# Two turns of the merge go ahead of the turns of the next unit's B and K on VectorE

## The chip, the cores and the metric

The kernel runs on one core of a Trainium2 chip. The metric is the device time of one execution in microseconds (us): 1092.59, the median of three runs (1092.51 to 1094.92).

The core's engines run side by side, each through its own queue of instructions in order: TensorE (PE in the profile; its weight loads are PEld), VectorE (DVE), ScalarE (ACT), GpSimd (POOL) and SyncE (SP), which issues nearly all DMAs. Semaphores tie them together.

## The reference

A recurrence over time steps (an attention block of 4 batches, 8 heads, 768 steps, head size 40), and behind it a mixture of four experts over all tokens:

```python
for t in range(S):
    y[:, :, t] = np.einsum('bhd,bhde->bhe', rt, state)
    Sa = np.einsum('bhde,bhe->bhd', state, at)
    state_decay = state * wt[:, :, None, :] - np.einsum('bhd,bhe->bhde', Sa, bt)
    state = state_decay + np.einsum('bhd,bhe->bhde', vt, kt)
...
x = attn_out.transpose(0, 2, 1, 3).reshape(B * S, H * D)      # 3072 tokens of 320
for e in range(E):                                            # 4 experts, F = 1024
    out += p[:, e:e + 1] * (np.maximum(x @ w1[e], 0.0) @ w2[e])
```

All data are 32-bit floats.

## The kernel before

**Units.** The recurrence is done in chunks of 64 steps. A unit is one chunk of one pair of batches, 16 heads at once; there are 12 chunks and 2 pairs, so 24 units, 0 to 23. Within a unit everything that doesn't depend on the state is made ahead (`within`, `substitute`, `merge`), and `step` then takes the state through. The mixture of the tokens of finished units is cut into pieces (`mix`, `gap`) that lie between the parts of the recurrence on TensorE and keep it busy. From unit 8 on (`BY_CHANNEL = 8`) B and K are loaded "raw", heads along the partitions, and VectorE turns them itself.

**What a unit does, in the order of its names.** G is the decay's running product (a turn of raw W at line 513, a scan at line 559), gp its reciprocal (line 575). AT is A turned (line 617) and multiplied by G (line 619); VT and RT are V and R turned (line 535). NT and KT are B and K turned (line 631, in two halves each; the turn itself is line 318) and multiplied by gp (lines 633 and 637). `pg` takes gp to another layout (line 641). `pc` is the product of V and R, masked into VC (line 492, called from line 604). `pfe` (line 656) is the product of NT and AT and gives F; `pe` (line 669) that of KT and AT. F holds triangular systems. `substitute` puts F's blocks into one tile and turns them into M (line 726), and GpSimd then solves by substitution in Z, in 16 rounds of one product and two sums (lines 756 and 773), some 50 instructions in a row. `merge` turns Z into Qc (line 784) and Qc into QTc (line 785), both on VectorE; GpSimd copies QTc into QT (line 791); TensorE makes `pY` from QTc (line 811) and, from its result and Qc, `pQ` (line 814), which completes QT. `step` begins with `prn` (products with the state; RH is added from it, line 835) and goes on with `psat`, which reads QT and RH.

**In TensorE's order**, which is that of the program, a late unit u has: `pg` and `pc` of unit u + 1; `pY` of unit u; `prn` of unit u; a piece of the mixture's first layer (`ph`); `pQ` of unit u; more of the mixture; `pfe` of unit u + 1; mixture, with `psat` and the rest of the step of u between.

**The mixture's buffers.** `ph` (first layer, two tiles) and `p` (second layer, `p431`, `p75`, `p26`) share three PSUM tiles (tag "mm"). ScalarE takes `ph` out as `hs` (line 969), VectorE adds halves of `hs` into sums `a` (line 1095) and takes `p` out into `osb` (lines 982 and 984). The recurrence's products share five PSUM tiles (tag "big").

**What sets the order on VectorE.** Instructions are placed by a scheduler that goes by readiness, program order and priority (`sooner` raises it, and VC has it raised from unit 7 on). `keep` holds an instruction in program order among those that are kept; Qc, QTc, the blocks, M and Z's first products on VectorE are. On top stand edges between named instructions: `noted` gives an instruction a name, and a list of pairs at the end (lines 1426 to 1435) says which of two goes first on VectorE, without a semaphore. The turns of B and K (line 631) have no name before the change; the products of K have ("K8" to "K23"). In program order the turns of B and K of unit u + 1 stand ahead of Qc of unit u, with pieces of the mixture between.

The lines that the change touches, and two that the steps need:

```python
                    turn_raw(t[:, i::2], n["raw" + x][:, NJ * i:NJ * i + NJ])                 # 631
        keep(noted(nc.vector.transpose(out=dealt(Qc[:]), in_=q.Z), "Qc", q.u))                # 784
    ahead_of_merge = [(f"K{u}", f"Qc{u - 1}") for u in range(BY_CHANNEL, NU)]                 # 1430
    ahead_of_merge += [(f"QTc{u - 1}", f"RH{u - 1}.{r}") for u in range(BY_CHANNEL, NU) for r in range(2)]
    ahead_of_merge += [(f"QTc{u - 1}", f"VC{u}.{r}") for u in range(BY_CHANNEL, NU) for r in range(2)]
```

Of the kernel before, what the change touches and what calls it, by code (L numbers as in the profile page):

```python
# [33 lines left out]
def kernel(  # L34
# [46 lines left out]
    NJ = H // 2  # L81
    NF = F // P
    NU = NC * B // 2
# [6 lines left out]
    def noted(ins, name, n=None, i=None):  # L90
        if n is None:
            n = sum(k.startswith(name) for k in made)
        key = f"{name}{n}" if i is None else f"{name}{n}.{i}"
        made[key] = ins
        if key in names:
            stated_order.append(ins)
        return ins
# [89 lines left out]
    def kept(name, shape, n, value=0.0, eng=nc.gpsimd, lo=0):  # L187
        tiles = []
        for i in range(n):
            t = const.tile(shape, FP32, name=f"{name}{i}")  # L190
            eng.memset(t[:, :, lo:shape[2]], value)
            tiles.append(t)
        turn = [0]

        def take():
            turn[0] += 1
            return tiles[(turn[0] - 1) % n]

        return take
# [6 lines left out]
    BY_CHANNEL = 8  # L206
    padded = {}
    for n, a_sum in enumerate(("a1", "a7", "a5", "a2")):
        t = padded["RV"[n % 2], n // 2] = sb.tile([P, H, 64], FP32, name="padded", tag=a_sum)
        nc.gpsimd.memset(t[:, :, D:64], 0.0)  # L210
    PAD = D + D - Q
    raw = {x: kept(f"raw{x}", [P, 2 * NJ, 2 * D], 1, float(x == "W"), nc.vector, PAD) for x in "WARV"}
# [103 lines left out]
    def turn_raw(out, t):  # L316

        return nc.vector.transpose(  # L318
            out=out.rearrange("p n (x two) -> p n two x", two=2),
            in_=t.rearrange("p n (two e) -> p n two e", two=2)[:, :, :, 0:Q],  # L320
        )
# [172 lines left out]
    def within(q):  # L494

        n = q.n
# [129 lines left out]
        if by_channel:  # L626
            NT = sb.tile([P, 2 * NJ, L], FP32, name="NT", tag="turned", bufs=3)
            KT = sb.tile([P, 2 * NJ, L], FP32, name="KT", tag="turned", bufs=3)
            for t, x in ((NT, "B"), (KT, "K")):
                for i in range(2):  # L630
                    turn_raw(t[:, i::2], n["raw" + x][:, NJ * i:NJ * i + NJ])
                if x == "B":
                    nc.vector.scalar_tensor_tensor(
                        out=t[:], in0=t[:], scalar=-1.0, in1=gp[:], op0=ALU.mult, op1=ALU.mult,
                    )
                else:
                    noted(nc.vector.tensor_tensor(out=t[:], in0=t[:], in1=gp[:], op=ALU.mult), "K", q.u)
# [569 lines left out]

    in_order[0] = True
    ws = [within(units[u]) for u in range(3)]
    norm = normalize()  # L1210
    keep_warm(16)
# [80 lines left out]
    substitute(units[2], nc.gpsimd)  # L1292
    mix(1)
    ws.append(within(units[3]))
    run(ws[3], 1)

# [5 lines left out]
    for u in range(1, NU):  # L1302
        in_order[0] = True
        q = units[u]
# [70 lines left out]
        if early:  # L1375
            run(m, 1)
        else:
            run(m, 1)
            run(s_next, 1)
            lead()  # L1380
            run(m, 1)
            if u + 3 < NU:
                ws.append(within(units[u + 3]))
                run(ws[u + 3], 1)
# [42 lines left out]
    turned_ahead = [("Qc6", "RT7"), ("RT7", "QTc6")]  # L1427
    turned_ahead += [("QTc6", x) for x in ("VC7.0", "VC7.1", "sum_w15", "sum_w16")]
    waits_of_scalar = [(f"SXc0.{n}", "RTc1.0") for n in range(4)]
    ahead_of_merge = [(f"K{u}", f"Qc{u - 1}") for u in range(BY_CHANNEL, NU)]  # L1430
    ahead_of_merge += [(f"QTc{u - 1}", f"RH{u - 1}.{r}") for u in range(BY_CHANNEL, NU) for r in range(2)]
    ahead_of_merge += [(f"QTc{u - 1}", f"VC{u}.{r}") for u in range(BY_CHANNEL, NU) for r in range(2)]
    in_second = [("Zr1.14", "out0"), ("out0", "Zm1.16")]
# [32 lines left out]
```

## Time and profile before

| | us |
|---|---|
| median of three runs | 1092.59 (1092.51 to 1094.92) |
| the profiled execution's own time | 1093.63 |
| its span, first to last instruction | 1091.9 |
| PE busy | 1055.7 (97%) |
| DVE busy | 797.3 (73%) |
| POOL busy | 524.4 (48%) |
| ACT busy | 343.8 (31%) |
| mean granted clock of TensorE, as a share of full speed | 0.998 |

How to read it: times in the views are microseconds from the span's start. A line of the timeline gives start, duration, engine, line of the kernel, operation, what is written from what, and behind "x" how many instructions are merged in it; in brackets stands the time that the engine was idle before it and what released it. A line of the waits gives the engine and what it wanted to run, what it waited for, the microseconds in sum, how often, and the longest. Ends of matmuls are modelled and overlap. The stage that the change touches runs from about 270 us (the merge of unit 7) to about 925 us (that of unit 22); a unit takes some 43 us there. From 965 us on only the mixture is left but for the last steps.

### The profile page before, as it was taken

To read this page: it belongs to the slowest core of one execution; us is meant where nothing else is said; L and a number is where in the kernel's file an instruction comes from. 1 tells how busy PE (TensorE), PEld (TensorE's weight loads), DVE (VectorE), ACT (ScalarE), POOL (GpSimd) and SP (SyncE) were. 2 spreads that over 40 slices of the span, in tenths; PEclk is the share of its full clock that TensorE was granted. 3 is DMA by queue.
4 is the path that set the end of the run, shared out by engine and by line. 5 is a ranking of instruction groups with operands and counts; after the bars stand their busy time and mean duration, and the time that the engine had idled before them with its cause. 6 is when DMAs were issued, how large, how long until landed. Compare 5 with 4: busy or idle time off the path is not lost.

```text
span 1091.9 us, 38473 instructions
## 1 busy us (share of the span) xinstructions
PE 1055.7 (97%) x16012; PEld 946.9 (87%) x16012; DVE 797.3 (73%) x1565; ACT 343.8 (31%) x942; POOL 524.4 (48%) x1312
## 2 busy tenths in 40 slices
PE   8999999999999999999999999999999999999998
PEld 7787878889889889898888898888988989988888
DVE  7886679897878877868868778678687786543343
ACT  3433344422333323323233333232333332321110
POOL 5116777756366364463572653643735537430000
PEclk9999999999999999999999999999999999999999
DMA  6775643435434453452463453443444443121220
GB/s 119 197 212 114 140 108 107 104 76 112 117 85 102 102 115 91 110 120 62 93 147 71 94 148 65 105 113 85 108 95 109 99 99 95 51 71 56 76 82 13
DMA packets 275989, 111.04 MB, mean 102 GB/s; under 512 B 230456, under 2 KB 255592, under 8 KB 275816
## 3 DMA queue, kind: packets, MB, share of 16 engines
q1 hardware_dynamic: 271832, 107.76, 41.7%
q8 instruction: 126, 2.06, 0.8%
q10 hardware_dynamic: 3984, 0.84, 0.4%
q14 instruction: 47, 0.39, 0.1%
HBM read 100.65 MB, written 3.93 MB: 96 GB/s over the span
## 4 chain that ended last, share of the span: by engine, by line
PE 62%; DVE 14%; POOL 12%; issue 4%; DMA 3%; SPq 3%; ACT 1%; DVEq 0%; POOLq 0%; ACTq 0%
PE ph L110 26%; PE p L110 23%; POOL Z L773 8%; POOL Z L756 4%; PE pdy L110 2%; DVE osb L984 2%; DVE M L726 2%; PE po L110 2%; PE prn L110 1%; PE psat L110 1%; PE pxr L110 1%; DVE a L1095 1%; PE pfe L110 1%; PE pY L110 1%; DVE KT L318 1%
## 5 line engine op out<-in xcount | busy, mean ns | idle before, releaser
L773 POOL TENSOR_TENSOR Z<-Z 128x31 f32<-128x31 f32 (+7 forms) x704 | 258.4, 367 | 55.1
L110 PE MATMUL ph<-xT,w1a 128*128 128x256 f32 (+3 forms) x1536 | 222.8, 374 | 2.8 <-DMA w1a<-in_moe_w_dram 2.0
L110 PE MATMUL ph<-xT,w1b 128*128 128x256 f32 (+3 forms) x1536 | 223.7, 374 | 1.5 <-DVE a L1095 0.5
L1095 DVE TENSOR_TENSOR a<-hs 128x512 f32<-128x512 f32 x220 | 152.2, 710 | 91.8 <-ACT hs L969 91.8
L969 ACT ACTIVATE hs<-ph 128x512 f32<-128x512 f32 (+1 forms) x208 | 116.8, 564 | 324.3 <-PE ph L110 323.9
L110 PEld LDWEIGHTS ph<-xT,w1a 128*128 128x128 f32 (+1 forms) x1536 | 169.4, 161 | 31.8 <-issue 9.0
L110 PEld LDWEIGHTS ph<-xT,w1b 128*128 128x128 f32 (+1 forms) x1536 | 169.9, 161 | 29.0 <-issue 6.4
L756 POOL TENSOR_TENSOR Z<-M,Z 128x62 f32<-128x62 f32 (+7 forms) x352 | 148.6, 422 | 79.7 <-DVE M L742 53.9
L984 DVE SCALAR_TENSOR_TENSOR osb<-p,gate,osb 128x320 f32<-128x320 f32 (+1 forms) x243 | 108.2, 483 | 84.0 <-PE p L110 80.0
L110 PE MATMUL p<-sums,a 128*128 128x160 f32 x1056 | 164.9, 299 | 0.0
L110 PEld LDWEIGHTS p<-sums,a 128*128 128x128 f32 x1056 | 152.8, 190 | 2.2
L719 POOL COPY below<-F 32x256 f32<-32x256 f32 x48 | 22.9, 478 | 201.9 <-ACT F L662 189.7
L110 PEld LDWEIGHTS p<-w,hs 128*128 128x128 f32 x704 | 98.6, 190 | 8.7 <-issue 7.5
L110 PE MATMUL p<-w,hs 128*128 128x160 f32 x704 | 104.9, 302 | 0.1
L110 PE MATMUL p<-w,a 128*128 128x160 f32 x704 | 102.8, 299 | 0.0
L110 PEld LDWEIGHTS p<-w,a 128*128 128x128 f32 x704 | 98.0, 190 | 0.0
L791 POOL COPY QT<-QTc 32x256 f32<-32x256 f32 x96 | 40.3, 420 | 99.2 <-DVE QTc L785 94.2
L889 ACT COPY RS<-pxr 64x256 f32<-64x256 f32 x88 | 32.2, 366 | 100.3 <-DVE SX L492 73.6
L575 DVE RECIPROCAL gp<-G 128x512 f32<-128x512 f32 x16 | 53.6, 3352 | 0.5
L700 ACT COPY EV<-pev 64x160 f32<-64x160 f32 x96 | 23.1, 286 | 83.5 <-PE pev L110 83.1
L726 DVE STREAM_TRANSPOSE M<-blocks 128x1024 f32<-128x1024 f32 x24 | 47.7, 1986 | 1.9 <-ACT blocks L714 0.3
L662 ACT COPY F<-pfe 128x256 f32<-128x256 f32 x48 | 15.6, 376 | 79.3 <-PE pfe L110 78.1
(167 smaller groups left out, 1420.6 us busy)
## 6 DMA issues: line engine op xcount, KB each, us to landing
w1a<-in_moe_w_dram SPq DMA_DIRECT2D x37, 512.0 KB
w1b<-in_moe_w_dram SPq DMA_DIRECT2D x37, 512.0 KB
w<-in_moe_w_dram SPq DMA_DIRECT2D x4, 1280.0 KB
w1a<-in_moe_w_dram SPq DMA_DIRECT2D x74, 64.0 KB
w1b<-in_moe_w_dram SPq DMA_DIRECT2D x74, 64.0 KB
out_dram<-osb SPq DMA_DIRECT2D x45, 80.0 KB
rawW<-in_w_dram SPq DMA_DIRECT2D x48, 72.0 KB
natV<-in_v_dram SPq DMA_DIRECT2D x42, 80.0 KB
```

What stands on the lines that cost most here:

```text
L110: return stated(nc.tensor.matmul(**k))
L575: pin(noted(nc.vector.reciprocal(out=gp[:], in_=G[:, :, 1:L + 1]), "1/gp", q.u))
L700: nc.scalar.copy(out=of_slot(q.EV[half(p)], i ^ p)[:, :, 0:D], in_=pev[i][half(p)])
L719: tc.keep_in_program_order(nc.gpsimd.tensor_copy(out=q.below[quarter(i)], in_=q.F[quarter(i), :, 0:Q]))
L726: ins = nc.vector.transpose(out=M[:], in_=cols)
L756: ins = eng.tensor_tensor(out=Z[:, 1:3, 0:n, j + 1:Q], in0=M[:, j:j + 2, None, j + 1:Q].to_broadcast([P, 2, n, m]), in1=Z[:, here, 0:n, j: ...
L773: eng.tensor_tensor(out=z[:, 0], in0=z[:, 0], in1=z[:, x], op=ALU.add)
L791: ins = nc.gpsimd.tensor_copy(out=q.QT[quarter(i), :, quarter(i % 2)], in_=QTc[quarter(i)])
L889: nc.scalar.copy(out=RS[half(s), x ^ s::2], in_=prs[x][half(s)].rearrange("p (j i) t -> p j i t", i=2),)
L969: ins = nc.scalar.activation(out=h[:, i * HF // 2:(i + 1) * HF // 2, 0:n], in_=ph[i][:], func=ACTF.Relu,)
L984: ins = nc.vector.scalar_tensor_tensor(out=to, in0=p, scalar=sc, in1=to, op0=ALU.mult, op1=ALU.add)
L1095: ins = nc.vector.tensor_tensor(out=t[:], in0=x, in1=y, op=op)
```

## The change

From unit 8 on, the four turns of a unit's raw B and K get names, Br8.0, Br8.1, Kr8.0, Kr8.1 and so on. The edge that put K's product of unit u ahead of Qc of unit u − 1 is taken out. Edges that put QTc of unit u − 1 ahead of the four turns of unit u are put in. The products of B and K follow their turns by their data. The edges from QTc to RH and VC stay.

```diff
             for t, x in ((NT, "B"), (KT, "K")):
                 for i in range(2):
-                    turn_raw(t[:, i::2], n["raw" + x][:, NJ * i:NJ * i + NJ])
+                    noted(turn_raw(t[:, i::2], n["raw" + x][:, NJ * i:NJ * i + NJ]), x + "r", q.u, i)
...
-    ahead_of_merge = [(f"K{u}", f"Qc{u - 1}") for u in range(BY_CHANNEL, NU)]
+    ahead_of_merge = [(f"QTc{u - 1}", f"{x}r{u}.{i}") for u in range(BY_CHANNEL, NU) for x in "BK" for i in range(2)]
     ahead_of_merge += [(f"QTc{u - 1}", f"RH{u - 1}.{r}") for u in range(BY_CHANNEL, NU) for r in range(2)]
     ahead_of_merge += [(f"QTc{u - 1}", f"VC{u}.{r}") for u in range(BY_CHANNEL, NU) for r in range(2)]
```

## The prediction

> **What bounds the kernel now.** I read the page's busy shares first, then the chain that ended last, then what TensorE (PE) waited for.
>
> ```profile
> PE 1055.7 (97%) x16012; PEld 946.9 (87%) x16012; DVE 797.3 (73%) x1565; ACT 343.8 (31%) x942; POOL 524.4 (48%) x1312
> ...
> PE 62%; DVE 14%; POOL 12%; issue 4%; DMA 3%; SPq 3%; ACT 1%; DVEq 0%; POOLq 0%; ACTq 0%
> ```
> PE is busy nearly throughout, yet only 62% of the chain is PE: VectorE (DVE) and GpSimd (POOL) hold 26%, so a serial ring through them is close behind. The waits of PE, longest first:
>
> ```profile
> PE pY L110 <- DVE QTc L785: 16.9, 16, 1.4
> PE pdy L110 <- issue: 2.1, 1, 2.1
> ```
> One wait stands out: pY, the first product of the merge, waits for the turn QTc, 16 times. One is unit 0's (0.41 us); the others are units 7 to 21, 16.5 us in sum: 0.79 and 1.40 in units 7 and 8, 1.07 to 1.30 in the thirteen after. **16.5 us is the ceiling** of what the change can take away. The timelines of DVE, then PE, around unit 14's merge:
>
> ```profile
> 575.66 0.67 DVE L984 SCALAR_TENSOR_TENSOR osb<-p,gate,osb 128x160 f32<-128x160 f32 x2
> 576.25 0.76 DVE L318 STREAM_TRANSPOSE NT<-rawB 128x256 f32<-128x256 f32 x2
> 577.04 0.69 DVE L633 SCALAR_TENSOR_TENSOR NT<-NT,gp 128x512 f32<-128x512 f32 x1
> 577.65 0.77 DVE L318 STREAM_TRANSPOSE KT<-rawK 128x256 f32<-128x256 f32 x2
> 578.45 0.69 DVE L637 TENSOR_TENSOR KT<-KT,gp 128x512 f32<-128x512 f32 x1
> 579.06 0.61 DVE L784 STREAM_TRANSPOSE Qc<-Z 128x256 f32<-128x256 f32 x1
> 579.71 0.45 DVE L785 STREAM_TRANSPOSE QTc<-Qc 128x256 f32<-128x256 f32 x1
> 580.07 0.74 DVE L492 COPY_PREDICATED VC<-mask_up,pc 128x256 f32<-128x256 int32 x2
> 581.48 0.71 DVE L318 STREAM_TRANSPOSE AT<-rawA 128x512 f32<-128x512 f32 x1 [0.67 <-PE prn L110]
> ```
> ```profile
> 580.29 0.59 PE L110 MATMUL pY<-QTc,below 64*64 64x64 f32 x13 [1.08 <-DVE QTc L785]
> ...
> 591.17 0.69 PE L110 MATMUL pfe<-NT,AT 40*64 40x64 f32 x32
> 591.68 1.10 PE L110 MATMUL ph<-xT,w1b 64*64 64x256 f32 x16
> ```
> PE's product pc ended at 579.21 and PE stood 1.08 until QTc was there. DVE was not idle: it ran the six operations on B and K (576.25 to 579.06, 2.81 us) ahead of Qc, though POOL had ended Z at 574.40. From 581.48 on, DVE runs without a pause to the M turn (594.32).
>
> **The change, part by part.** No instruction is added or removed, and no DMA, POOL, PE or ScalarE instruction is moved. Two kinds of edges on DVE change: Qc no longer stands behind the K product, and the four turns of B and K stand behind QTc. So 2.81 us of DVE work go from in front of Qc/QTc (1.09 us from Qc's start to QTc's end) to behind them, in 16 units.
>
> *Gain at pY.* Without that work Qc may start at the end of the four osb additions or at the end of Z, whichever is later. In unit 14: Qc 576.25, QTc ends 577.34, pY can start 0.14 later (as 580.29 after 580.15) and is then held by pc, 579.21. The 1.08 go. In units 7 and 8 Qc already waited 1.03 us for Z, so nothing is gained there; in 9 to 21 it is at most 14.3 us.
>
> *What the turns cost behind QTc.* NT is read by pfe, 12 us after QTc, KT by pe, 20 us after; both are far enough. The raw buffers come free 1.1 us later, but SyncE issues the next load into them long after (522.80 against the turn at 488.64), so that costs nothing; a load that lands late costs less than before, since its turn is later (unit 13's K turn waited 0.13 us). What matters is the rest of DVE's queue: VC, AT, RH, G, scan, 1/gp, the hidden-state sums and the two p75 osb additions stand behind the turns. PE's first ph product after pfe needs PSUM that those two additions release: they end at 591.06 and ph starts at 591.68, so 0.5 us are in hand after the 0.13 of the signal. PE now comes 1.08 earlier; DVE comes 0.67 earlier, because the wait of AT for prn is covered by the turns. 0.5 + 0.67 − 1.08 is about 0.1: unit 14 gains its whole 1.08, and nothing is left over. **Any wait of DVE at Qc for Z therefore comes back at ph.**
>
> *Whether Qc waits for Z.* In unit 15 it does. POOL's timeline:
>
> ```profile
> 619.17 0.52 POOL L773 TENSOR_TENSOR Z<-Z 128x8 f32<-128x8 f32 x2
> 623.13 1.73 POOL L791 COPY QT<-QTc 32x256 f32<-32x256 f32 x4 [3.45 <-DVE QTc L785]
> ```
> Z ends at 619.68, the osb additions at 619.18. After the change unit 15's M turn comes 0.67 earlier with DVE, so Z ends at 619.01, while PE and the additions come 1.08 earlier (618.10). Qc starts at 619.05, 2.86 before its old 621.91; the turns behind it and the vanished AT wait give 2.81 − 0.67 = 2.14 back; the p75 additions end 0.72 earlier, at 633.20, and ph starts at 633.30 instead of 634.53: 1.23 earlier in all, 0.15 of it unit 15's own. Unit 16: Z 0.72 earlier (661.20), Qc 661.24, 3.67 earlier, additions 1.53 earlier, ph 2.05 earlier: 0.82 of its own. The other even units (10 to 20) keep 0.8 to 1.14 in the same way. So a pair of units gains about **1.0 us, not 2.2**, and 10 to 21 are six pairs: −6.0 us.
>
> *The start of the stage loses.* In units 7 and 8 Qc is released by Z, so the ring Z → Qc → QTc → DVE's queue → M → Z is the bound, and the turns are now inside it:
>
> ```profile
> 274.91 0.62 DVE L784 STREAM_TRANSPOSE Qc<-Z 128x256 f32<-128x256 f32 x1 [1.03 <-POOL Z L773]
> 275.56 0.45 DVE L785 STREAM_TRANSPOSE QTc<-Qc 128x256 f32<-128x256 f32 x1
> 275.93 0.74 DVE L492 COPY_PREDICATED VC<-mask_up,pc 128x256 f32<-128x256 int32 x2
> 277.87 0.32 DVE L835 TENSOR_TENSOR RH<-prn,EV 128x160 f32<-128x160 f32 x1 [1.21 <-PE prn L110]
> ```
> Only the 1.21 us before RH cover 2.81: M of unit 8, and so Qc 8, comes 1.6 us later. Unit 8 adds another 1.6, less the 0.95 that Qc 9 used to start after Z's end: Qc 9 is 2.3 late. In unit 9 the 2.14 of the turns stand against a slack of 1.07: ph 3.5 us late.
>
> **Sum:** +3.5 − 6.0 + about 0.2 in units 11 and 22 = −2.3 us. The profiled execution took 1093.63 (span 1091.9); that is 1.04 above the median of the runs shown, 1092.59. 1093.63 − 2.3 = 1091.3, by the median **1090.3 us**. Bounds: VC's place is unknown, and whether the other waits of PE at ph (0.27 to 1.30 us in the six odd units 9, 11, 13, 17, 19 and 21, put down mostly to DMAs of w1) move along: I let them move with the unit before. If they don't bind at all, −4.0; if AT's turn falls behind the p75 additions, as it stood in units 7 and 8, −5.0.
>
> A rule weighed here: POOL's pair of Z additions at 128x69 took 0.74 us (at 602.98) and the one at 128x68 took 1.26 (at 606.97), when DVE began the sums of two inputs. The Trainium skill, "SBUF — State Buffer", section "Who interferes with whom", says that a VectorE instruction with two SBUF inputs contends with GpSimd's reads. By that rule the N product (0.69) leaves Z's tail in units 9, 11 and 13, where Z ended during or just after it, and N falls on the QT copies instead, which is against the change, though psat reads QT only 12 us later. By the rule, as an estimate, the sum would be −2.3 less up to three times 0.7, −4.4; by the rows alone it is −2.3.
>
> **Rivals.**
> 1. *VC stands right behind QTc (slower).* VC reads pc. The stated edges put VC behind QTc but not behind the turns, and VC has a raised priority. pc now ends 1.9 us after QTc (579.21 against 577.34), so with less than 1.9 us of turns between them DVE waits for PE. Placed in front of all six, VC starts 0.15 after pc, the p75 additions end 0.15 + (591.06 − 580.07) − 0.67 + 2.81 = 13.28 after pc, ph starts at 13.4 instead of 12.47: +0.93 a unit in 10 to 21, some of it inside the DMA waits: with the start +13: 1105.6. For it: the priority. Against: pc isn't ready when QTc ends, so a placement by readiness takes the turns first.
> 2. *VC amid the turns, behind N.* It still waits a little, and a pair gains about 0.5: the start is just paid back, +0.8: 1093.4.
> 3. *The cover holds.* Free DVE operations are placed anew, ph is not held and units 7 and 8 lose little: up to −14.3: 1078.3. For it: DVE is idle 27% of the span. Against: from 581.48 to the M turn it isn't idle at all.
> 4. *Nothing changes*, because the new names don't bind: the key made of "Br", the unit and the half is the one that the edges use, so I give this almost nothing.
>
> **How the numbers follow.** Forecast 0.40, rival 1 0.27, rival 2 0.18, rival 3 0.15 (rival 4 within the second). A measurement tells 0.3% (3.3 us) from no change. Faster by more: rival 3 and 0.13 of the forecast (its lower end): 0.28. Slower by more: rival 1 and 0.02 of rival 2: 0.29. Within: 0.43. The range reaches from a partly held cover (1082) to rival 1 (1106) and leaves out rival 3's end.
>
> **What would show it.** Right: pY's wait for QTc is gone but for units 7 and 8 (and some odd ones); Qc in odd units waits for Z; new PE waits of some 0.8 us on "DVE osb" at the first ph in odd units; Qc 9 some 2 us later than 361.06; a pair of late units near 84.9 us instead of 85.85. Rival 1: VC idle on PE pc, a unit above 43.5 us. Rival 3: units of 41.8 us. What would make me wrong: DVE's order between QTc and M differing from before in more than these eight operations.

## The result, and the profile after

The changed kernel took 1089.17 us (median of 14 runs, 1080.98 to 1091.22) against 1093.32 for the kernel before, run beside it on the same chip (14 runs, 1089.94 to 1099.04). The ratio, of the means, is 0.9946, with an interval of [0.9925, 0.9967] (the medians alone give 0.996): a little faster. The forecast of 1090.3 and its range hold. The mechanism behind it holds only in part, as the runs below show.

The profiled execution of the changed kernel took 1089.61, its span is 1087.6. Of the 4.0 us between the two profiled executions, 2.6 arose ahead of the merge of unit 6: the trace of before has a pause of 2.1 us there ("pdy, issue" in its waits), which that of after lacks and which came back in one of the experiments (2.2 us in w1_pinned). The change isn't its cause: all queues have the same order in both kernels up to 268 us. From pY of unit 7 to pY of unit 22, the stage that the change touches, TensorE took 649.63 before and 648.42 after. I use this **stage time** below, since it leaves such pauses out. It is that of one execution; why this one gained only 1.2 us, where the means of the runs are 5.9 apart, is open but for the clock (below).

The page of after, engines and chain:

```profile
PE 1057.9 (97%) x16012; PEld 948.8 (87%) x16012; DVE 804.4 (74%) x1565; ACT 342.9 (32%) x942; POOL 538.7 (50%) x1312
...
PE 66%; POOL 13%; DVE 9%; SPq 4%; issue 4%; DMA 3%; ACT 1%; DVEq 0%; ACTq 0%; POOLq 0%
```

VectorE's share of the chain fell from 14% to 9%, SyncE's queue rose from 3% to 4%, and TensorE's own from 62% to 66%. The waits of TensorE say the same thing (engine and what it wanted, what it waited for, microseconds in sum, times, longest):

```profile
PE ph L110 <- DMA w1a<-in_moe_w_dram: 11.2, 5, 3.8
PE ph L110 <- DMA w1b<-in_moe_w_dram: 4.4, 4, 1.8
...
PE pY L110 <- DVE QTc L785: 0.4, 1, 0.4
```

The wait of pY is gone to the last 0.4 of unit 0. In its place stand 15.6 us in which the first-layer products `ph` wait for their weights w1, where before had 2.0 (and 1.8 at the same place put down to ScalarE and VectorE). They are in odd units: 2.3, 0.9, 3.9, 1.4, 3.0, 1.8 and 2.0 us in units 9, 11 and so on to 21, and 0.25 in unit 7. The even units from 10 on now run in 41.54 us from pY to pY (before, 42.85 to 43.07); the odd ones from 9 on take 42.9 to 47.4. The timelines of VectorE and TensorE in unit 15 of the kernel after, which answer to those shown of unit 14 before:

```profile
617.08 0.62 DVE L784 STREAM_TRANSPOSE Qc<-Z 128x256 f32<-128x256 f32 x1 [1.09 <-POOL Z L773]
...
618.93 0.77 DVE L492 COPY_PREDICATED VC<-mask_up,pc 128x256 f32<-128x256 int32 x2 [0.76 <-PE pc L110]
619.61 0.76 DVE L318 STREAM_TRANSPOSE NT<-rawB 128x256 f32<-128x256 f32 x2
...
635.10 1.97 DVE L726 STREAM_TRANSPOSE M<-blocks 128x1024 f32<-128x1024 f32 x1
```
```profile
629.51 0.69 PE L110 MATMUL pfe<-NT,AT 40*64 40x64 f32 x32
631.64 1.35 PE L110 MATMUL ph<-xT,w1b 64*64 64x256 f32 x13 [1.44 <-DMA w1b<-in_moe_w_dram]
```

Three things are to be seen. Qc waits 1.09 us for Z. VC stands right behind QTc and waits for pc (in odd units from 9 on; in even ones it stands behind the two B turns, in unit 10 behind B's product too, and waits up to 1.30). And between the B turns and M the AT turn and its product, which stood there before (581.48 in unit 14), are missing: the scheduler has moved them behind M from unit 8's stage on, K's turns (from unit 9 on) behind G's turn or the scan, and SyncE's loads of rawA and natV to other places in its queue. The stated edges let two turns go ahead; in the end some 180 of VectorE's 1565 instructions and 80 of SyncE's 1344 issues stand at another place. Orders of TensorE, ScalarE and GpSimd are the same.

Why w1 comes late shows in SyncE's issues, of after and then of before (start, duration of the issues, and how many):

```profile
617.62 9.78 SPq L935 DMA_DIRECT2D xT<-Y  x12
627.50 1.65 SPq L397 DMA_DIRECT2D w1b<-in_moe_w_dram  x3
```
```profile
620.90 8.95 SPq L935 DMA_DIRECT2D xT<-Y  x12
629.95 1.68 SPq L397 DMA_DIRECT2D w1b<-in_moe_w_dram  x3
```

From 603.51 on SyncE issues almost without a pause: w1a, rawW, rawB, four stores, rawK, the tokens, then twelve moves of xT at 0.7 to 0.8 us each, and only then the next w1. Before, pY's stall of 1.08 us a unit brought `ph` of unit 15 to 634.53, and it found its load landed. After, TensorE is there at 630.2 and waits until 631.64. Counted from pY of unit 7, TensorE is done with `pfe` 0.4 to 2.9 us earlier than before in the odd units 9 to 19, while the last issue of w1 ahead of it comes between 0.7 us earlier and 0.7 later.

A second loss goes with these waits: TensorE's granted clock. Over the stage it is 1.000 before and 0.992 after. The trace of after has three stretches of 3.4 us at half of full speed there, from 371.9, 545.9 and 890.7, each beginning within 1.4 us of the end of the wait for w1 in units 9, 13 and 21; they take up to 5.1 us (half of their length). A window inside that of unit 13, and before it one of before behind its own wait in unit 13 (window, its length, TensorE's busy time and instructions, granted clock, share and GB/s of the DMAs):

```profile
549.00:552.00 3.00, 3.00 (x86) 1.00 0.72 203
```
```profile
546.00:549.00 3.00, 3.00 (x73) 0.50 0.79 218
```

Less its waits, unit 13 took 42.2 us before and 43.6 after. The longest wait of before in the stage is 1.4 us, and no stretch at half speed follows it.

### The profile page after: what moved, and what is told of

The parts are those of the page before. It is cut to its first block, busy times and chain, and to the rows that moved or that the text cites. A ratio compares the mean times of both kernels' runs of the same rounds, so it can differ in the third digit from the quotient of the medians.

```text
span 1087.6 us, 38520 instructions
## 1 busy us (share of the span) xinstructions
PE 1057.9 (97%) x16012; PEld 948.8 (87%) x16012; DVE 804.4 (74%) x1565; ACT 342.9 (32%) x942; POOL 538.7 (50%) x1312
## 4 chain that ended last, share of the span: by engine, by line
PE 66%; POOL 13%; DVE 9%; SPq 4%; issue 4%; DMA 3%; ACT 1%; DVEq 0%; ACTq 0%; POOLq 0%
PE ph L110 30%; PE p L110 22%; POOL Z L773 8%; POOL Z L756 5%; SPq L935 4%; PE pdy L110 2%; DMA w1a<-in_moe_w_dram 2%; PE psat L110 2%; PE po L110 2%; DVE M L726 1%; PE pxr L110 1%; DMA w1b<-in_moe_w_dram 1%; PE prn L110 1%; PE pc L110 1%; DVE gp L575 1%
## 5 line engine op out<-in xcount | busy, mean ns | idle before, releaser
L110 PE MATMUL ph<-xT,w1a 128*128 128x256 f32 (+3 forms) x1536 | 225.1, 378 | 11.2 <-DMA w1a<-in_moe_w_dram 11.2
L719 POOL COPY below<-F 32x256 f32<-32x256 f32 x48 | 32.0, 667 | 207.3 <-ACT F L662 150.4
L791 POOL COPY QT<-QTc 32x256 f32<-32x256 f32 x96 | 42.8, 446 | 66.8 <-DVE QTc L785 50.3
L726 DVE STREAM_TRANSPOSE M<-blocks 128x1024 f32<-128x1024 f32 x24 | 47.4, 1973 | 2.4 <-DVE blocks L714 0.5
```

The costliest lines, as they stand in the source:

```text
L110: return stated(nc.tensor.matmul(**k))
L719: tc.keep_in_program_order(nc.gpsimd.tensor_copy(out=q.below[quarter(i)], in_=q.F[quarter(i), :, 0:Q]))
L726: ins = nc.vector.transpose(out=M[:], in_=cols)
L791: ins = nc.gpsimd.tensor_copy(out=q.QT[quarter(i), :, quarter(i % 2)], in_=QTc[quarter(i)])
```

## The experiments

Two theories were tested. **A**: what the change frees at pY is taken back at `ph` by SyncE's train of issues in front of w1. **B**: the ring Z, Qc, QTc, VectorE's queue with the B and K turns in it, M, Z bounds the units by itself. All runs were compared with the kernel before on the same chip; ratios are to it.

**1. w1_first: the next w1 load ahead of the xT moves, in every second unit.**

```diff
-                    nc.sync.dma_start(out=xT[...], in_=Y[...])
+                    move = lambda ...: nc.sync.dma_start(out=out, in_=in_)
+                    if q.bp == 0 and q.u >= EARLY:
+                        late_x.append(move)      # issued behind the next w1 piece
+                    else:
+                        move()
```

> The changed kernel; only on SyncE, from unit 6 on in every second unit, the next load of w1 (three issues) goes ahead of the twelve xT issues instead of behind them. Theory A (the changed kernel is held by SyncE's train of issues: the first ph of an odd unit waits for a load of w1 that stands behind it): the waits of PE for DMAs of w1, 15.6 us in the changed kernel's profile, fall under 4 us, and the time is 8 to 13 us below the changed kernel, some 1077 to 1081 us, ratio to before 0.983 to 0.988. Theory B (what I forecast: VectorE's queue behind QTc and the ring through GpSimd hold it): the same waits come back as waits for VectorE, the time moves by less than 2 us, ratio near 0.994.

Measured: 1115.66, ratio 1.0197 [1.0172, 1.0221], stage 675.88. The DMA waits are gone, but pY waits 32.6 us for QTc. Ten stretches at half clock take up to another 20.5 us of the stage. The run doesn't tell A from B, for the edit changed VectorE's order too. VectorE in a late even unit of it:

```profile
781.52 1.43 DVE L722 COPY blocks<-F 32x256 f32<-32x256 f32 x2
782.98 3.35 DVE L583 RECIPROCAL gp<-G 128x512 f32<-128x512 f32 x1
786.25 1.88 DVE L734 STREAM_TRANSPOSE M<-blocks 128x1024 f32<-128x1024 f32 x1
```

The scheduler put the reciprocal of 3.35 us between the blocks and M, so in the ring. Hence run 5.

**2. k_behind_m: K's turns behind the second product of M.**

```diff
+    ahead_of_merge += [(f"Z2{u}", f"Kr{u}.{i}") for u in range(BY_CHANNEL, NU) for i in range(2)]
```

> The changed kernel; only the two turns of K are held back further, behind M's first products on VectorE (K's product follows), so that 1.45 us of VectorE's work leave the way from QTc to M in every late unit. Theory B: the ring gets up to 1.45 us shorter in each of some 14 units, the time falls by 5 us or more, ratio 0.990 or lower. Theory A: M and Z come earlier, PE still waits for the loads of w1, the time moves by less than 1.5 us, ratio 0.993 to 0.996.

Measured: 1089.24, ratio 0.9971 [0.9953, 0.9989], stage 645.40. The ring is relaxed (M starts 0.9 us behind F's copy in units 8 to 21, where after had 1.6 to 4.6; the scheduler moved the reciprocal behind M too), yet the time is that of the change: the w1 waits stay (7.1 + 4.5 us, and 3.3 at the same place put down to ACT's blocks). The ring alone isn't what holds the kernel after.

**3. both_w1_k: both edits on the kernel after.**

> The two edits above together. Theory A: as w1_first, or up to 2 us better where VectorE comes next, 1075 to 1081 us. Theory B: as k_behind_m, ratio 0.990 or lower, no better for the order on SyncE. If both are bounds close to each other, only this one falls clearly, to 0.983 or lower, while each alone moves by less than 4 us.

Measured: 1066.53 (1065.71 to 1068.63), ratio 0.9751 [0.973, 0.9772], stage 624.52. Engines and chain of this kernel:

```profile
PE 1049.6 (99%) x16012; PEld 941.3 (88%) x16012; DVE 796.8 (75%) x1565; ACT 341.3 (32%) x942; POOL 536.8 (50%) x1312
...
PE 79%; POOL 12%; DVE 5%; issue 3%; ACT 1%; SPq 0%; DMA 0%; DVEq 0%; POOLq 0%; ACTq 0%
```

Every unit takes 41.5 to 42.1 us, TensorE is busy 99% and SyncE and the DMAs have left the chain. This beats both kernels. On the kernel after (0.9946) K's turns alone bring nothing (0.9971); with the w1 load they bring the rest, for either bound hides the other. VectorE's order isn't exactly that of run 2 here, so the two shares are read from run 5.

**4. before_w1_first: run 1's edit on the kernel before** (all orders but SyncE's are those of before).

> The kernel before; only the order on SyncE as in w1_first. Theory A: in the kernel before the pY waits give the loads time, so only its own waits for w1 (3.4 us in its profile) can go: 1 to 3.4 us faster, ratio 0.997 to 0.999, and the pY waits of 16.5 us stay. Theory B: no change, ratio 0.999 to 1.001.

Measured: 1086.53, ratio 0.9933 [0.9912, 0.9955], stage 644.36. The w1 waits of before go, pY's waits stay (18.1 us in sum). So the w1 load alone brings about as much as the whole change (0.9946).

**5. w1_pinned: run 1's edit on the kernel after, VectorE's and ScalarE's orders written out as they are in after.** Only SyncE's order differs (in w1 and xT, and in six loads of rawA).

```diff
+    order_of_after = "... Qc14 QTc14 Br15.0 Br15.1 VC15.0 VC15.1 N15 RH14.0 ...".split()
+    ahead_of_merge += [*zip(order_of_after, order_of_after[1:])]
```

> The kernel after with the next w1 load issued ahead of the twelve xT moves in every second unit, and with the orders of VectorE, ScalarE, GpSimd and TensorE held exactly as in the kernel after: only SyncE's order differs. (The run w1_first let VectorE's order change with it.) Theory A: in the kernel after, SyncE's train of issues alone takes the gain of the odd units back; the late w1 also makes hs late, the sums of hs stand in front of the blocks on VectorE, and so M is 4.2 us behind F's copy there instead of 1.9. With the load early both go: DMA waits of TensorE at ph (15.6 us in units 9 to 21) gone, M 2 us behind F's copy in all units, units 41.5 to 41.9 us, time 1071 to 1077. Theory B: VectorE's queue with the K turns in it bounds the kernel after anyway, as it did in w1_first: the DMA waits turn into waits of pY for QTc of about the same size, units 42.5 us or more, time 1085 or above.

Measured: 1078.28, ratio 0.9867 [0.9852, 0.9883], stage 635.23. This lies between A and B, and both are seen at work. The w1 waits are gone, worth 0.8% (0.9867 against 0.9946), so SyncE's train did take most of the gain back. Of its 15.6 us 10.8 return as waits of pY (first line below; then VectorE at Qc of unit 16). Within the stage, 13.2 us shorter than in after, TensorE waits 7.0 us less, and the stretches at half clock, up to 5.1 us, are gone:

```profile
PE pY L110 <- DVE QTc L793: 10.8, 9, 1.8
```
```profile
655.11 0.62 DVE L792 STREAM_TRANSPOSE Qc<-Z 128x256 f32<-128x256 f32 x1 [3.10 <-POOL Z L781]
```

The ring adds up: Qc to M 18.04 in unit 15, 3.73 to Z's start, 21.79 of Z, makes 43.6; in unit 16 it is 15.40 + 3.75 + 22.03, or 41.2; the pair 84.8, and pY to pY gives 84.8. One part of A as I had put it is wrong: M stays 4.2 us behind F's copy in odd units though hs is no longer late. VectorE's queue does that by itself.

**6. qc_only: the change as the prediction worked it out.** VectorE's order of before, with only Qc and QTc in front of the six operations.

```diff
+    order_of_vector = "... Qc14 QTc14 Br15.0 Br15.1 N15 Kr15.0 Kr15.1 K15 VC15.0 VC15.1 AT16 RH14.0 ...".split()
+    ahead_of_merge += [*zip(order_of_vector, order_of_vector[1:])]
```

> The forecast's own model of the change: the order of VectorE of the kernel before, in which only Qc and QTc of units 7 to 22 stand in front of the six B and K operations of the next unit (VC behind all six, AT and its product in front of M, as before). By the prediction's steps: 1090 to 1091.5 on the scale of a kernel before at 1093.6, pY's waits gone but in units 7 and 8, Qc 9 two us late, TensorE held some 0.8 us by VectorE's osb additions at the first ph in odd units. Theory A: the same waits for w1 as in the kernel after, 1.5 to 4 us at the first ph of odd units, on a DMA, none above 0.2 on osb; time 1086 to 1091.

Measured: 1143.4, ratio 1.0443 [1.0422, 1.0464], stage 702.88, 50 us slower, as no theory had it. SyncE, then VectorE, behind the merge of unit 14:

```profile
591.63 9.43 SPq L935 DMA_DIRECT2D xT<-Y  x12
601.10 0.48 SPq L296 DMA_DIRECT2D rawA<-in_a_dram  x1
```
```profile
603.24 0.71 DVE L318 STREAM_TRANSPOSE AT<-rawA 128x512 f32<-128x512 f32 x1 [5.16 <-DMA rawA<-in_a_dram]
```

I had left SyncE's order to the scheduler, and it put the last piece of rawA behind the xT train, while AT's turn stands ahead of RH and the sums on VectorE. AT waited 40.5 us in 6 units. The run tells more of SyncE than of the change; run 9 holds SyncE too.

**7. qc_only_w1: run 6 with the w1 load ahead.**

> qc_only with the next w1 load ahead of the twelve xT moves in every second unit; the orders of VectorE, ScalarE, GpSimd and TensorE are those of qc_only. Theory A: without the w1 waits the ring of Z, Qc, QTc, VectorE's queue, M and Z shows: AT and its product (1.4 us) and the six operations (2.81) are inside, so M follows Qc by some 16.7 us, with 3.7 to Z's start and 21.7 of Z a unit takes 42.1 to 42.5: waits of pY for QTc of 0.5 to 1 us in most units, time 1078 to 1084. The prediction's step 2: the osb additions hold the first ph instead, pY isn't held, and a pair takes 84.9 us, time about 1088. If neither binds: 41.6 us a unit, 1070.

Measured: 1126.27, ratio 1.0302 [1.0286, 1.0318]. It has the same fault and decides nothing.

**8. vc_first: rival 1, VC right behind QTc in every unit.**

```diff
+    ahead_of_merge += [(f"VC{u}.{r}", f"Br{u}.{i}") for u in range(BY_CHANNEL, NU) for i in range(2) for r in range(2)]
```

> The kernel after with VC placed right behind QTc, ahead of the B turns, in every unit (it stands there in the odd ones from 9 on already): the placement of rival 1. Rival 1's price: +0.93 us a unit for the units that it is new in, and 1105.6 for all on the scale of a kernel before at 1092.6. Theory A: VectorE then waits for pc some 1 to 1.9 us in even units too, but the odd units have slack in the w1 wait: +0.3 to +1.0 us for each of the six even units 10 to 20, so 1090 to 1096. If the wait is hidden everywhere: 1089.

Measured: 1090.43, ratio 0.9975 [0.9963, 0.9988], stage 647.72. VectorE waits 13.9 us for pc, as in after (14.3, 16 times), and the stage is no longer for it. Rival 1's placement costs some 0.3% against after (0.9975 to 0.9946, by the ends of the intervals at most 0.6%), not 13 us against before.

**9. qc_alone: run 6 with SyncE's order held as in before too.** Nothing but Qc and QTc has moved.

> The kernel before with one thing moved: Qc and QTc of units 7 to 22 in front of the six B and K operations, VC and AT behind them. VectorE's order is otherwise that of before, and so are the orders of TensorE, ScalarE, GpSimd and SyncE (in qc_only SyncE's order had changed too: the last piece of rawA was issued behind the twelve xT moves and the AT turn waited 5.2 us for it). This is the change as the prediction worked it out. By its steps: 2.3 us less than before, 1090 to 1091.5 on the scale of 1093; a pair of late units 84.9 us; at the first ph of odd units 0.8 us on VectorE's osb additions; Qc 9 two us late. Theory A (SyncE's train): odd units lose the gain to w1 loads, 1.5 to 4 us each, on a DMA, time 1088 to 1092. Theory C: AT's turn, with 2.81 us more in front of it, is still ahead of its rawA load or the sums come late, and the kernel loses as qc_only did: above 1100.

Measured: 1094.58 (1093.37 to 1097.13), ratio 1.0010 [0.9997, 1.0023], stage 651.96. **The move alone brings no gain in time.** pY's waits shrink from 16.9 to 3.1 us, and what they leave is taken by w1 in odd units (up to 3.7 us), by the additions in front of `ph`, and by the clock: at the waits for w1 of 3.7 and 2.2 us the trace has 10.2 us at half speed, worth up to 5.1, where before has none. Without them the stage would be 646.8, 2.8 us under that of before. In the 12 runs the mean granted clock is 0.9934, in the 19 of before beside them 0.9959; over the spans that is an estimated 2.8 us, more than the 1.2 us by which the mean time of qc_alone lies above that of before. So without the clock the move would gain an estimated 1.6 us, give or take 1.0.

**10. qc_alone_w1: run 9 with the w1 load ahead** (SyncE's order that of before_w1_first).

> qc_alone with the w1 load ahead of the twelve xT moves in every second unit; all orders but VectorE's are those of before_w1_first (1086.5), whose pY waits were 1.08 a unit. By the prediction's step 2 and 3 (Qc waits for Z in odd units and the osb additions then hold ph): 84.9 us a pair, 1086 minus 2 to 6, so 1080 to 1084, with waits on osb or on QTc of about 1.5 us a pair. If only w1 held the units: 41.6 us each, about 1070. If the longer queue in front of M costs more than the moved Qc gains: above 1087.

Measured: 1088.33, ratio 0.9957 [0.9941, 0.9973], stage 644.81 against 644.36 in before_w1_first: again no gain from the move, now without w1 and without a stretch at half clock in the stage (before_w1_first has one, worth up to 1.7). TensorE's waits, and then VectorE's p75 addition and the product that it holds up, in unit 14:

```profile
PE ph L110 <- issue: 11.3, 14, 1.1
PE pY L110 <- DVE QTc L793: 4.7, 4, 2.0
```
```profile
590.49 0.38 DVE L994 SCALAR_TENSOR_TENSOR osb<-p,minus_gate,osb 128x160 f32<-128x160 f32 x1
```
```profile
590.97 0.87 PE L110 MATMUL ph<-xT,w1b 64*64 64x256 f32 x11 [0.65 <-issue]
```

The trace names no releaser ("issue"), but the product starts 0.10 after the addition ends. This reads as the PSUM release that the prediction had put there.

**11. at_behind_m: the kernel before with only AT's turn and product moved behind M.**

> The other half of what happened to VectorE's order: the kernel before with the AT turn and its product (0.71 and 0.63 us) moved from in front of RH and the sums to behind the second product of M, in units 9 to 23, as in the kernel after; Qc stays behind the B and K operations, all other orders are those of before. pY's waits of 1.08 us come from the six operations in front of Qc and not from Z, so by every theory they stay: 1092 to 1094. If the AT place is worth something by itself (RH and VC's followers earlier, Z 1.3 us earlier): 1088 to 1091.

Measured: 1122.56, ratio 1.0268 [1.0245, 1.0292], stage 679.42. SyncE, and VectorE at the B turns of unit 15:

```profile
548.07 1.66 SPq L397 DMA_DIRECT2D w1a<-in_moe_w_dram  x3
557.96 0.32 SPq L296 DMA_DIRECT2D rawA<-in_a_dram  x1
```
```profile
584.81 0.77 DVE L318 STREAM_TRANSPOSE NT<-rawB 128x256 f32<-128x256 f32 x2 [1.77 <-DMA rawB<-in_b_dram]
```

The next load of rawA needs the buffer that AT's turn reads. Issued at its old place in the queue it stands still for 8 us until the turn at its new place is done, and with it all of SyncE (67.8 us in 11 such waits); rawB, rawR and rawV land late. Of the 29.8 us that the stage is longer, up to 10.2 are again TensorE at half clock.

**12. qc_and_at: both moves, SyncE as before.**

> Both together on the kernel before: Qc and QTc in front of the six operations, the AT turn and its product behind M; SyncE, ScalarE, GpSimd and TensorE as before. By the prediction's sum with a ring that is 1.3 us shorter: Z is there when Qc wants it, a pair gains 2.2 us, time 1079 to 1081. Theory A: the odd units' w1 waits take at least half of that back, 1086 to 1090, as in the kernel after (ratio 0.995). If qc_alone loses and this one doesn't, the planner's new place for AT is what made the change worth its gain.

Measured: 1117.21, ratio 1.0224 [1.0198, 1.0251], stage 671.08. The same stall, with VT waiting for rawV and rawR (38.3 and 23.3 us).

Runs 9, 11 and 12 against the change itself say that the 0.5% isn't the move's alone: that gives 1.001, AT behind M on the old SyncE order loses 2%, and only with SyncE's rawA loads moved as well, as the scheduler did by itself, is it 0.995. How much of this belongs to AT's place, VC's and K's was not taken apart further.

**Where the stage time goes**, in microseconds of the profiled executions. "Half clock" is half the length of the stretches at half speed, an upper bound, since TensorE also waits in part of some.

| run | stage | waits of TensorE | half clock | the rest, its work |
|---|---|---|---|---|
| before | 649.6 | 20.3 | 0 | 629.3 |
| after | 648.4 | 15.9 | 5.1 | 627.4 |
| w1_first | 675.9 | 30.5 | 20.5 | 624.9 |
| both_w1_k | 624.5 | 0.4 | 0 | 624.1 |
| before_w1_first | 644.4 | 17.6 | 1.7 | 625.1 |
| w1_pinned | 635.2 | 8.9 | 0 | 626.3 |
| qc_alone | 652.0 | 17.0 | 5.1 | 629.9 |
| qc_alone_w1 | 644.8 | 13.5 | 0 | 631.3 |
| qc_only | 702.9 | 51.6 | 23.9 | 627.4 |
| at_behind_m | 679.4 | 38.2 | 10.2 | 631.0 |

## Why the prediction held in number and not in mechanism

**pY's wait as the ceiling of the change: held.** It went from all units, in the kernel after from 7 and 8 as well.

**"No DMA, POOL, PE or ScalarE instruction is moved": failed, and is the main error.** The prediction named "DVE's order between QTc and M differing from before in more than these eight operations" as what would make it wrong, and so it came. A scheduler that goes by readiness places everything anew around an edge. SyncE's order changed along. The run that is the prediction's own model, qc_alone, gives 1.0010, or +1.1 us, where the model gave −2.3. Some 2.8 us of this difference are TensorE's clock, for which the prediction had no term; less these the move gains an estimated 1.6 us. So the sum isn't far off as a count of waits and work, but its terms are, on both sides, as the next points show.

**Qc waits for Z in odd units, "a pair gains about 1.0 us": the size failed.** In qc_alone_w1 Qc waits for Z in every unit (line below, of unit 14), and a pair of units 10 to 21 takes 85.91 us, as in before_w1_first, not 84.9:

```profile
576.67 0.63 DVE L792 STREAM_TRANSPOSE Qc<-Z 128x256 f32<-128x256 f32 x1 [0.99 <-POOL Z L781]
```

I had taken Qc to M as 17.40 in even and 16.81 in odd units (15.26 and 14.67 in before, and the 2.14); measured are 18.06 and 17.70, 1.55 more for the pair, against which the way from M to Z's end was only some 0.6 shorter. Operations that now stand beside others took longer. Groups of VectorE from 270 to 930 us, in before and then in qc_alone (microseconds in sum, mean ns of one):

```profile
L714 DVE COPY blocks<-F 32x256 f32<-32x256 f32 x30 | 12.3, 409 | 0.2
L633 DVE SCALAR_TENSOR_TENSOR NT<-NT,gp 128x512 f32<-128x512 f32 x16 | 11.1, 695 | 0.5
```
```profile
L714 DVE COPY blocks<-F 32x256 f32<-32x256 f32 x30 | 20.4, 678 | 0.2
L633 DVE SCALAR_TENSOR_TENSOR NT<-NT,gp 128x512 f32<-128x512 f32 x16 | 13.2, 826 | 0.6
```

N's product now lies beside GpSimd's copies of QT, in all 16 units. The two block copies of a unit lay mostly beside GpSimd's copies into `below` before (24 of 30, 340 ns in the mean; the 6 beside GpSimd's product n_tok took 686); now 25 of 30 lie beside its products n_tok and k_tok and take 642 and 799. VectorE, then GpSimd, in qc_alone behind the merge of unit 14:

```profile
593.94 1.53 DVE L714 COPY blocks<-F 32x256 f32<-32x256 f32 x2
```
```profile
593.26 1.18 POOL L722 TENSOR_TENSOR n_tok<-n_tok,decay 128x320 f32<-128x320 f32 x1
594.41 0.91 POOL L722 TENSOR_TENSOR k_tok<-k_tok,decay 128x320 f32<-128x320 f32 x1
```

Together that is 0.13 + 2 × 0.27, or 0.67 us a unit, and all of it in the ring. The mean GpSimd copy of QT grew from 393 to 481 ns. The Trainium skill, "SBUF — State Buffer", section "Who interferes with whom", says that copies and two-input operations of VectorE can contend with GpSimd. These rows agree, though no run moved these operations alone, and so does the Z that the N product left (unit 7: 22.37 before, 21.54 in qc_alone). The prediction used this rule for the gain at Z, and by it went to −4.4; it had set the same rule's price on the other side at nothing. The other side was larger.

**"Any wait of DVE at Qc for Z comes back at ph" through the osb additions: right where it can be seen, and hidden in the kernel after.** In qc_alone_w1 it is 14 waits of 0.8 us. In after AT and its product (1.3 us) are out of the way, the additions end 0.46 us ahead of `ph` or more from unit 11 on, and w1 holds it instead. I had let the w1 waits "move with the unit before": this is the term that failed. They don't move with TensorE, since SyncE's train takes its own time: TensorE came earlier and w1 hardly did, the waits of TensorE at `ph` for w1 grew from 2.0 to 15.6 us, and the clock took up to 5.1 more.

**The start loses 3.5 us: failed.** (The terms given for unit 9, 2.3 + 2.14 − 1.07, make 3.4.) pY of unit 7 to pY of unit 9 took 86.14 before, 84.44 after and 86.16 in qc_alone. In qc_alone Qc to M in unit 7 grew by 1.0, where 1.6 was foreseen, and a shorter Z paid it back. In after the scheduler had taken AT's product, which stood between unit 9's sums and M, away.

**Rival 1** described the order of half the units, and its price was wrong: VectorE's wait for pc seems to lie inside time that w1 takes from the odd units anyway. **Rival 3**, units of 41.8 us, is what the even units do.

So it was luck that the sum of −2.3 came near the measured −4.2 (medians; 5.9 by the means): its own model gained no time when run alone, and the gain came with a new order that the forecast had left out.

## What to carry to other kernels

A bound that stalls an engine in every unit gives time to all queues behind it; ahead of removing it, lay the time line of each DMA queue against the earlier arrival, issue by issue, and not only the semaphores. Where a scheduler places instructions, an edge between two is a new plan for all: read the orders of all queues, the one that issues the DMAs among them, and pin them where an effect is to be measured. Two bounds within 1 us of each other a unit hide each other, and only an experiment that lifts both shows what either is worth. And read the granted clock stage by stage: a mean of 0.994 against 0.998 looks like nothing, and was up to 5 us in the stage here, more than the effect that was looked for.

## What the runs showed of the hardware

A DMA issue on SyncE took 0.43 us (rawV, rawR) to 0.72 us (xT) in the median of its kind in the stage of after, and bytes don't set it: in the train shown the three of w1 (512 and twice 64 KB) took 0.55 each, the twelve of xT (20 KB and less) 0.8. During the xT train the DMA engines of the kernel after were nearly idle (40 slices of 1 us from 600 on, in tenths; from 619 to 628 it is 0 or 1):

```profile
DMA  0000289975643663665110101000478947997523
```

So it is the time to issue the xT moves that made w1 late, and not the transfer. The Trainium skill, "DMA: Bandwidth & Descriptors", section "Issuing engines are not separate DMA queues", says that starting DMAs from several engines saves only the sequencer's time to start them, which is usually small relative to the DMA itself. Here this time was the bound; a second issuing engine was not tried.

A load that waits for its buffer holds up all loads behind it on SyncE (8 us at a time in at_behind_m), so that an operation on VectorE, moved back by some 16 us, cost 2.7% through a queue that the move did not touch.

TensorE's clock was halved for 3.4 us, or two or three times that, around waits of TensorE. In the stage of all fourteen traces every such stretch begins during a wait of 1.6 us or more or within 1.7 us of its end. Not every such wait has one: that of 3.0 us in unit 17 of after has none. The stages of before, w1_pinned and qc_alone_w1, whose longest waits are 1.4, 1.8 and 1.5 us, have no stretch at half clock. In the 14 runs of after, time and clock go together: the three fastest (1080.98 to 1084.90 us) had a mean granted clock of 0.997 or 0.998, the other eleven 0.992 to 0.995.
